# A state-space layer beside a gated MLP: the compute instructions in another order, twelve copies on the other engine

## The chip, the cores and the metric

One Trainium2 chip, one core of it. The core has TensorE (PE, matmuls; PEld is its loading of weights), VectorE (DVE), ScalarE (ACT), GpSimd (POOL) and SyncE (SP, which here only starts transfers). The metric is the device time of one execution in microseconds; lower is better. The time before is a median of three runs; the traces come from one profiled execution.

## The reference

The input is x, 2048 tokens of 512 channels. After a layernorm two branches read it, and both are added to the input:

```python
xn = _layernorm(x, axis=-1)
return x + _A_ref(xn, ...) + _B_ref(xn, ...)

# A: state-space convolution, 128 complex modes for each channel
logdA = dt * A                                  # dt = exp(log_dt)
P = jnp.exp(logdA[:, :, None] * l[None, None, :])
K = jnp.einsum("dn,dnl,dn->dl", Cc, P, dB).real
y = irfft(rfft(u, padded) * rfft(K, padded))[:L] + u * Dskip
# B: gated MLP, F = 1792
h = _sigmoid(x @ w_gate) * (x @ w_up)
return h @ w_down
```

Everything comes in and goes out as bf16.

## The kernel before, in words

The kernel is a plan of 927 numbered operations. An operation is a short Python function that issues one instruction or a few on one engine, or one transfer. `_Plan.add` (L265) numbers them in the order in which the code names them. `_Plan.run` (L291) gives them out in the order of the list `ORDER` (L206), and each engine executes its own in that order, waiting where an input isn't ready. An operation may also take a buffer out of a pool and give one back (`acq`, `rel`); which buffer of the pool it gets is settled by `ORDER` too, first freed, first used. The pool "s" has two pairs of PSUM banks of 128x1024 f32, the pool "gu" four single banks.

`_Plan.copy` (L279) makes a copy that either engine can do: on DVE as `tensor_copy` (L286 in the profile) when its number stands in the tuple `ON_DVE` (L204), else on ACT as an activation (L288). Two other tuples, `UEV` and `ON_ACT`, do the like for other operations; they are the same before and after.

The work, with the numbers that matter here:

- *Layernorm.* Four groups of 512 tokens: statistics on DVE (L542, L543), a small part on POOL (L481, L482, or L492), then `fn2` on DVE (L501, L502) and the scaling on either (L549, L554). Transposed tokens go to `xnT`.
- *Gated MLP.* Four groups of 512 tokens. A gate tile is four matmuls (`fg`, L1045), an up tile four (`fu`, L1069); ACT takes the sigmoid (L1057), up tiles come out through ACT (L1084) or not, and DVE multiplies (L1089, L1094). Then four down-projections of 14 matmuls for each group (L1123).
- *Power tables.* A ladder of squares (L669 on ACT, L676 and L678 on DVE) gives the powers of the modes. In four chunks c of 128 channels tables G and H are filled by complex products on DVE (L737, L738, L742, L743), squares on ACT (L792) and eight small seed copies for each chunk (L777, operations 194 to 201, 240 to 247, 287 to 294, 333 to 340). Matmuls of G with H (L823) give the kernel's samples.
- *The convolution in the frequency domain.* x goes through a first transform (L695), out to a scratch in DRAM and back. Then come two passes p of 256 channels with eight units u each. A unit is: a matmul into a pair (`fm`, L885); an eviction of the pair (L889); a swap of halves into the other half of the partitions, by transfers in pass 0 and for three units of pass 1, and by four DVE copies (L898) for the five others; a matmul of the kernel's spectrum (`fk`, L911) and its eviction (L913); products on DVE (L916, L920); the inverse transform (`fv`, L935) into a pair; its eviction (L939); and a store to the scratch `v_scr`.
- *The end.* When all units are stored, `reload` (L972) reads `v_scr` back in parts: five transfers on SP, two on ACT, and later one more on SP behind a first output store. For the first three groups of tokens `final` (L999) makes 2 x 4 matmuls into a pair (L994), and DVE adds the MLP's part (L1020). For the last group the matmuls go on top of the down-projection in its bank (L994 and L997), and DVE adds the input (L1143); its fourth block is done in two halves. Each result goes out with a transfer.

Around the places that the prediction speaks of, the rows of the engines are these (numbers of operations; p, u are pass and unit):

| engine, place | before | after |
|---|---|---|
| DVE near 155 to 168 us | 430, 445 (L916 of p0 u6, u7), 850, 906 (L1094, L1089), 446 (L920 of p0 u7), 431 (L920 of p0 u6), 498 (L898 of p1 u3), 370, 560 (L898 of p1 u2) | 445, 430, 431, 906, 585, 446, 433, 850, 498, 370, 560 |
| ACT there | 585 (eviction, L889, p1 u7), 571, 882, 874, 433 (eviction, L939, p0 u6), 448 (L939, p0 u7), 497 (L889, p1 u3), 861, 890 | 571, 882, 448, 874, 497, 890 |
| PE there | 873, 570, 584, 881, 892, 432 (`fv` p0 u6), 447 (`fv` p0 u7), 889 (gate), 496 (`fm` p1 u3) | 881, 584, 570, 873, 892, 432, 447, 889, 496 |
| PE in the tail | 908, 911 (down-projection of blocks 1 and 2 of the last group), 832, 829 (finals), 915 (down-projection of block 3), 909, 921, 912, 916, 919 (convolution added to blocks 1, 4, 2, 3, 4), 838, 835, 920, 841, 844, 922 | 908, 911, 829, 832, 909, 912, 915, 916, 919, 838, 835, 920, 841, 844, 921, 922 |

Before as after, 432 writes into the pair that 585 empties, and 496 into the pair that 433 empties.

Of the kernel before, what the change touches and what calls it, by code (L numbers as in the profile page):

```python
# [182 lines left out]
def _consts():  # L183
# [17 lines left out]
                MAB=f(np.stack([quads(MA[by], True), quads(MB[by], True)], axis=2)), E=f(_build_E(M2, by).reshape(128, NU // 2, 2, NKT, 128).transpose(1, 0, 2, 3, 4)))  # L201

UEV = (6, 7, 10, 11, 12, 13, 14, 15, 16, 17, 18, 19, 22, 23, 24, 25, 26, 27, 28, 29, 30, 31, 32, 33, 34, 35, 36, 37, 38, 39, 40, 41, 44, 45, 46, 47, 52, 53, 54, 55,)
ON_DVE = (86, 89, 104, 106, 121, 122, 123, 137, 138, 184, 194, 195, 198, 199, 201,)  # L204
ON_ACT = (2,)
ORDER = [  # L206
# [40 lines left out]

class _Op:
    __slots__ = ("alt", "tab", "eng", "cost", "fn", "prio", "acq", "rel", "dma", "left", "users", "ready", "start", "done", "seq", "mode")
# [8 lines left out]
class _Plan:  # L258
# [20 lines left out]
    def copy(self, nc, cost, out, in_, *args, **kw):  # L279

        get = lambda v: v() if callable(v) else v
        dve = len(self.ops) in ON_DVE

# [35 lines left out]
def kernel(  # L319
# [209 lines left out]
    def layernorm(i0, i1, prio):  # L529
# [15 lines left out]
        for i in range(i0, i1):  # L545
            dve = i < LN_ACT or len(pl.ops) in ON_DVE
            if not dve:
# [110 lines left out]
    def f_cast(cur, k, dve):  # L658
        for p in range(NP):
            if dve:  # L660
                V.tensor_copy(out=W[p][:, k], in_=cur[:, :, DW * p:DW * p + DW])
            else:
                S.activation(out=W[p][:, k], in_=cur[:, :, DW * p:DW * p + DW], func=ACT.Identity)
    cast_prev = [None, None]
    for k in range(12):
        cur = wt[(2 * k) % 3]
        sq, nxt = wt[(2 * k + 1) % 3], wt[(2 * k + 2) % 3]
        if k < 11:
            s_op = pl.add("ACT", 0.95, lambda cur=cur, sq=sq: S.activation(out=sq, in_=cur, func=ACT.Square),  # L669
                          [cur_op] + W_op[-1:], PLAD + k * 0.01)  # L670
        dve = len(pl.ops) in ON_DVE
        c_op = pl.add("DVE" if dve else "ACT", 1.04, lambda cur=cur, k=k, dve=dve: f_cast(cur, k, dve), [cur_op],
# [540 lines left out]
```

## Time and profile before

| | |
|---|---|
| median of 3 runs | 215.39 us (213.83 to 215.43) |
| profiled execution, span from first to last instruction | 213.6 us |
| granted TensorE clock | 1.000 |
| busy: PE, DVE, ACT | 204.2, 191.3, 177.1 us |
| DMA | 42.61 MB, mean 199 GB/s |

A busy PE is not PE at its peak: the end of a matmul is modelled and overlaps the next one. A line of a timeline has the start in us, the time from the first start to the last end of instructions merged in it, engine, line, operation, output and inputs with their shapes, and in brackets the idle time before it with what ended it. A group's line has, behind the bar, busy us and the mean ns of one, and behind the second bar the idle us just before its instructions. A wait's line has the total us, how often, and the longest.

### The profile page before, as it was taken

What the parts mean: (1) busy time and instruction counts of PE and PEld (TensorE: products, weight loads), DVE (VectorE), ACT (ScalarE), POOL (GpSimd) and SP (SyncE); (2) the same over time, 40 slices, a digit from 0 to 9 for tenths busy, and PEclk for the clock granted to TensorE, in tenths of its full rate; (3) what the DMA queues carried; (4) which work ended last, traced back from release to release, by engine and by line L of the source; (5) the groups of instructions that cost most, each with busy time, mean ns of one, the idle gap of its engine ahead of it and who ended that gap; (6) DMA issues with size and microseconds to landing.
All of it is one profiled execution on the core that took longest, in us unless ns stands there. A gap on an engine that the chain in (4) does not pass through costs nothing.

```text
span 213.6 us, 4875 instructions
## 1 busy us (share of the span) xinstructions
PE 204.2 (96%) x1838; PEld 102.9 (48%) x1864; DVE 191.3 (90%) x406; ACT 177.1 (83%) x284; POOL 27.8 (13%) x32
## 2 busy tenths in 40 slices
PE   7989999999999999999999999999999999999992
PEld 2654444444443444445436555544654645644482
DVE  4799999999979999999999999999992999990494
ACT  5699999999999999997999989978989998870000
POOL 2120026008980000002000000001200000000000
PEclk9999999999999999999999999999999999999999
DMA  5999269124464236967965878787967799698864
GB/s 148 316 383 381 100 147 324 61 98 147 110 126 104 76 105 229 213 191 151 249 185 141 228 202 237 215 221 175 202 188 208 217 284 274 141 357 218 240 213 172
DMA packets 52377, 42.61 MB, mean 199 GB/s; under 512 B 16641, under 2 KB 44546, under 8 KB 52354
## 3 DMA queue, kind: packets, MB, share of 16 engines
q1 hardware_dynamic: 50658, 40.30, 63.9%
q0 software_dynamic: 864, 1.57, 4.8%
q10 hardware_dynamic: 832, 0.43, 0.8%
q8 instruction: 14, 0.23, 0.5%
q14 instruction: 9, 0.07, 0.1%
HBM read 24.99 MB, written 12.85 MB: 177 GB/s over the span
## 4 chain that ended last, share of the span: by engine, by line
PE 41%; DVE 40%; POOL 6%; DMA 4%; issue 4%; ACT 3%; DVEq 0%; SPq 0%; ACTq 0%
PE pair L911 8%; PE bank L1045 7%; PE bank L1123 7%; PE bank L1069 7%; DVE big L737 6%; DVE big L738 6%; POOL ln_ve_b L481 5%; PE pair L935 5%; DVE big L742 4%; DVE big L743 4%; DVE stats L542 3%; DVE hT_sb L1094 3%; DVE hT_sb L1089 3%; DVE big L678 2%; DMA big<-v_scr 2%
## 5 line engine op out<-in xcount | busy, mean ns | idle before, releaser
L288 ACT ACTIVATE big<-pair 128x1024 bf16<-128x1024 f32 x64 | 64.5, 1039 | 6.9 <-DVE big L920 1.7
L1069 PE MATMUL bank<-xnT,wu_sb 128*128 128x512 bf16 x214 | 52.9, 379 | 1.7 <-issue 0.6
L1123 PE MATMUL bank<-wd_sb,hT_sb 128*128 128x512 bf16 (+1 forms) x231 | 50.6, 367 | 0.5 <-issue 0.2
L1045 PE MATMUL bank<-xnT,wg_sb 128*128 128x512 bf16 (+1 forms) x191 | 45.6, 370 | 1.0 <-issue 0.5
L1045 PEld LDWEIGHTS <-wg_sb 128*128 128x128 bf16 x240 | 22.5, 98 | 25.0 <-issue 3.2
L1123 PEld LDWEIGHTS <-hT_sb 128*128 128x128 bf16 x238 | 22.4, 98 | 24.9 <-issue 1.6
L1069 PEld LDWEIGHTS <-wu_sb 128*128 128x128 bf16 x224 | 20.7, 98 | 27.5 <-issue 5.4
L1057 ACT ACTIVATE hT_sb<-bank 128x512 bf16<-128x512 f32 x48 | 28.2, 627 | 0.7 <-PE bank L1045 0.7
L737 DVE TENSOR_TENSOR big<-big 128x1024 bf16<-128x1024 bf16 (+4 forms) x40 | 26.7, 667 | 0.2
L738 DVE TENSOR_TENSOR big<-big 128x1024 bf16<-128x1024 bf16 (+4 forms) x40 | 26.5, 663 | 0.0
L1084 ACT ACTIVATE us_sb<-bank 128x512 bf16<-128x512 f32 x40 | 23.6, 616 | 0.6 <-DVE hT_sb L1089 0.3
L911 PE MATMUL pair<-big 128*128 128x256 bf16 x160 | 19.8, 273 | 0.0
L916 DVE TENSOR_TENSOR big<-big 128x2048 bf16<-128x2048 bf16 x16 | 19.3, 1217 | 0.1
L911 PEld LDWEIGHTS <-big 128*128 128x128 bf16 x160 | 15.4, 98 | 4.7 <-issue 0.8
L481 POOL TENSOR_SCALAR ln_ve_b<-mvb 128x4 bf16<-128x4 bf16 x3 | 13.0, 4323 | 34.1 <-DVE mvb L543 34.1
L742 DVE TENSOR_TENSOR big<-big 128x512 bf16<-128x512 bf16 (+4 forms) x40 | 16.5, 413 | 0.2
L743 DVE TENSOR_TENSOR big<-big 128x512 bf16<-128x512 bf16 (+4 forms) x40 | 16.5, 412 | 0.0
L792 ACT ACTIVATE sq_sb<-big 128x256 bf16<-128x256 bf16 (+2 forms) x20 | 13.2, 658 | 1.6 <-DVE big L743 1.5
L1089 DVE TENSOR_TENSOR hT_sb<-hT_sb,us_sb 128x1024 bf16<-128x1024 bf16 x20 | 13.5, 683 | 0.0
L935 PE MATMUL pair<-big 64*64 64x512 bf16 (+1 forms) x256 | 13.1, 327 | 0.0
L898 DVE COPY big<-big 32x1024 bf16<-32x1024 bf16 x20 | 8.4, 418 | 4.5 <-ACT big L288 4.2
L288 ACT ACTIVATE big<-big 128x256 bf16<-128x256 bf16 x30 | 12.4, 452 | 0.0
(99 smaller groups left out, 229.8 us busy)
## 6 DMA issues: line engine op xcount, KB each, us to landing
big<-c_E SPq DMA_DIRECT2D x13, 320.0 KB, 4.4
z_scr<-big SPq DMA_DIRECT2D x16, 256.0 KB, 2.9
big<-z_scr SPq DMA_DIRECT2D x16, 256.0 KB, 4.2
v_scr<-big SPq DMA_DIRECT2D x16, 256.0 KB, 3.2
big<-big SPq DMA_DIRECT2D x44, 64.0 KB, 3.3
big<-in_A_u_dram SPq DMA_DIRECT2D x4, 512.0 KB, 9.1
wu_sb<-in_B_w_up_dram SPq DMA_DIRECT2D x2, 896.0 KB, 10.8
wd_sb<-in_B_w_down_dram SPq DMA_DIRECT2D x1, 1792.0 KB, 9.0
```

Source lines behind the costliest of these rows:

```text
L288: nc.scalar.activation(out=get(out), in_=get(in_), func=ACT.Identity)
L481: P.tensor_scalar(out=q["ve_b"], in0=mvb[:, s, 1], scalar1=EPS, scalar2=None, op0=ALU.add)
L737: V.tensor_tensor(out=wide(outp), in0=wide(lo), in1=mre, op=ALU.mult)
L738: V.tensor_tensor(out=wide(tb()), in0=wide(lo), in1=mim, op=ALU.mult)
L742: V.tensor_tensor(out=outp[:, :, 0], in0=outp[:, :, 0], in1=tb()[:, :, 1], op=opr)
L743: V.tensor_tensor(out=outp[:, :, 1], in0=outp[:, :, 1], in1=tb()[:, :, 0], op=opi)
L911: T.matmul(two(sk)[:, o:o + DW], es()[:, g, kt, :], kTv[p][:, :, kt, :], start=kt in (0, NKT - 1), stop=kt >= NKT - 2)
L935: T.matmul(two(sv)[o:o + 64, DW * (2 * g + y):2 * DW * (g + 1)], mab[b:b + 64, 2 * u + g, q, :], pq()[b:b + 64, q, ch] if y else pp()[b:b ...
L1045: T.matmul(bank(sl, k % 2)[:, c0:c1], w[:, kt, k * 128:(k + 1) * 128], xnT[:, grp, kt, c0:c1], start=(kt == 0), stop=(kt == KT - 1))
L1057: S.activation(out=hT_sb[:, hs.idx, k % 2, :], in_=bank(sl), func=ACT.Sigmoid)
L1069: T.matmul(bank(sl), wu_sb[:, kt, k * 128:(k + 1) * 128], xnT[:, grp, kt, :], start=(kt == 0), stop=(kt == KT - 1))
L1123: T.matmul(bank(po)[:, 0:c[1] - c[0]], hT_sb[:, hts[k // 2].idx, k % 2, jj * 128:(jj + 1) * 128], wd_sb[:, k, c[0]:c[1]], start=first and ...
```

## The change

All operations stay; 12 copies change the engine, and `ORDER` is another permutation of the same 927 numbers. The 168 transfers that SP starts are in the same order as before, and so are those of ACT and POOL among themselves. Of the copies, 198 and 201 go from DVE to ACT; 196, 200, 240, 243, 247, 287, 333, 336 (seeds of the tables H, L777), 433 and 585 go from ACT to DVE. POOL's row differs in one place: the table's constant (193) now stands behind the last layernorm group's part (134).

```diff
-ON_DVE = (86, 89, 104, 106, 121, 122, 123, 137, 138, 184, 194, 195, 198, 199, 201,)
+ON_DVE = (86, 89, 104, 106, 121, 122, 123, 137, 138, 184, 194, 195, 196, 199, 200, 240, 243, 247, 287, 333, 336, 433, 585,)
 ON_ACT = (2,)
 ORDER = [
...
-    444, 902, 867, 429, 361, 511, 513, 348, 340, 865, 362, 419, 430, 445, 363, 557, 510, 365, 873, 868, 850, 364, 366,
-    368, 570, 584, 373, 372, 367, 585, 533, 881, 571, 882, 906, 545, 892, 586, 874, 446, 589, 431, 369, 432, 433, 447,
-    889, 496, 448, 574, 857, 497, 587, 558, 861, 498, 370, 588, 597, 890, 522, 449, 860, 559, 883, 560, 523, 434, 371,
...
+    868, 438, 363, 816, 895, 425, 364, 439, 445, 365, 512, 881, 494, 430, 431, 906, 366, 323, 521, 511, 584, 570,
+    873, 513, 419, 557, 510, 368, 585, 446, 892, 432, 571, 433, 372, 367, 882, 533, 447, 448, 850, 889, 874, 496,
+    558, 545, 586, 497, 498, 890, 589, 369, 370, 559, 560, 860, 857, 861, 883, 884, 522, 523, 590, 574, 587, 588,
...
-    555, 872, 863, 600, 819, 879, 531, 876, 556, 532, 601, 878, 602, 888, 880, 908, 821, 911, 825, 832, 833, 829, 828,
-    824, 826, 915, 909, 921, 822, 823, 830, 831, 827, 912, 916, 910, 919, 838, 834, 835, 913, 917, 914, 839, 836, 920,
-    923, 918, 841, 844, 922, 840, 924, 842, 845, 837, 843, 925, 846, 926]
+    553, 554, 555, 568, 819, 529, 888, 530, 531, 556, 877, 532, 872, 879, 600, 878, 863, 876, 821, 825, 373, 828,
+    880, 601, 908, 911, 829, 602, 824, 830, 826, 822, 832, 833, 909, 912, 823, 910, 915, 913, 916, 917, 831, 827,
+    919, 838, 839, 835, 836, 920, 923, 834, 841, 842, 914, 844, 918, 921, 922, 840, 924, 845, 837, 843, 846, 925,
+    926]
```

69 rows, old and new, of the table ORDER are left out of this document.

## The prediction

> **What bounds the kernel now.** I read the table of stages first, since a busy share over the whole span hides which engine sets the pace where; then the waits, then the timelines of the two places where an engine stands still. In the table each row is a stretch, and an engine's first number is its busy time in it.
>
> ```profile
> PE 204.2 (96%) x1838; PEld 102.9 (48%) x1864; DVE 191.3 (90%) x406; ACT 177.1 (83%) x284; POOL 27.8 (13%) x32
> ```
> ```profile
> core 0: us, PE busy (x) PEld busy (x) DVE busy (x) ACT busy (x) POOL busy (x), PEclk, DMA share, GB/s
> 12.00:112.00 100.00, 98.58 (x749) 44.53 (x758) 98.14 (x231) 97.14 (x169) 23.23 (x18) 1.00 0.61 175
> 112.00:160.00 48.00, 47.42 (x592) 25.69 (x601) 47.62 (x95) 43.34 (x67) 2.26 (x3) 1.00 0.78 202
> 160.00:164.00 4.00, 3.82 (x51) 1.58 (x44) 0.05 (x1) 4.00 (x7) 0.00 (x0) 1.00 0.81 235
> 164.00:190.00 26.00, 25.34 (x257) 14.64 (x261) 25.45 (x42) 22.59 (x28) 0.00 (x0) 1.00 0.83 241
> 190.00:214.00 24.00, 19.37 (x149) 11.27 (x149) 12.21 (x20) 2.32 (x4) 0.00 (x0) 1.00 0.72 218
> ```
> Three engines are full at once. From 12 to 160 us PE, DVE and ACT all work over 90% of the time, at the full clock (1.00). So another order can win only what is idle now, and can lose much more. What PE, the fullest, waited for at its three big groups (the number behind the bar) is small:
>
> ```profile
> L1069 PE MATMUL bank<-xnT,wu_sb 128*128 128x512 bf16 x214 | 52.9, 379 | 1.7 <-issue 0.6 <-ACT hT_sb L1057 0.2 <-DVE hT_sb L1094 0.2
> L1123 PE MATMUL bank<-wd_sb,hT_sb 128*128 128x512 bf16 (+1 forms) x231 | 50.6, 367 | 0.5 <-issue 0.2
> L1045 PE MATMUL bank<-xnT,wg_sb 128*128 128x512 bf16 (+1 forms) x191 | 45.6, 370 | 1.0 <-issue 0.5 <-ACT xnT L572 0.3
> ```
> That is 1.7 + 0.5 + 1.0 = 3.2 us, 1.5% of the span: about the most that an order can take out of PE in the middle. DVE has one hole, in the row 160 to 164 (0.05 busy), while ACT is full there (4.00 of 4.00). In the waits it is the first of these lines, against the longest wait for a neighbour that DVE had before 160 us:
>
> ```profile
> DVE big L898 <- ACT big L288: 4.2, 1, 4.2
> DVE ln_ri_f L501 <- POOL ln_sd_b L482: 1.2, 1, 1.2
> ```
> After the hole DVE runs 25.45 of 26 us without a pause, to the last product of the convolution; then come that unit's last matmul and copy, the store, the reload, and the final adds. So two things set the end: when the exchange copies (L898) after the hole can start, and how the last 15 us are ordered.
>
> **The twelve copies.** Ten of them are small seeds of the power tables (128x256 bf16; 196, 200, 240, 243, 247, 287, 333, 336 to DVE, 198 and 201 to ACT), so DVE gets six more. A seed on DVE shows 0.27, but the next instruction starts 0.13 us later, here at 54.07 behind 53.94:
>
> ```profile
> 53.94 0.27 DVE L286 COPY big<-big 128x256 bf16<-128x256 bf16 x1
> 54.07 1.22 DVE L737 TENSOR_TENSOR big<-big 128x2048 bf16<-128x2048 bf16 x1
> ```
> Six of them cost DVE 6 x 0.13 = 0.8 us (6 x 0.27 = 1.6 at most, nothing if each fell into a gap). I take 0.8, as DVE has almost no gap up to 160 us. It arrives at the hole that much later, and the hole swallows it.
>
> The two others are evictions of a PSUM pair (128x1024 f32): the spectrum of pass 1, unit 7 (585) and the result of pass 0, unit 6 (433). On ACT one is 1.04 us. DVE has never done this one; the nearest rows are an add from such a pair and a copy of bf16 from a pair:
>
> ```profile
> L288 ACT ACTIVATE big<-pair 128x1024 bf16<-128x1024 f32 x64 | 64.5, 1039 | 6.9 <-DVE big L920 1.7 <-PE pair L935 1.2 <-PE pair L885 1.0
> L1020 DVE TENSOR_TENSOR big<-pair,glu_sb 128x1024 bf16<-128x1024 f32 x4 | 4.7, 1216 | 6.5 <-PE pair L994 6.5
> L574 DVE COPY xnT<-pair 128x1024 bf16<-128x1024 bf16 x1 | 0.7, 684 | 0.0
> ```
> So each costs DVE 0.7 to 1.2 us; I take 1.2, since its source is f32 in PSUM as in the add. Both, 2.4 us, stand in DVE's new row exactly before the L898 copy that ends the hole. If the hole were not there they would cost 2.4.
>
> **Through the hole, step by step.** DVE, ACT and PE before:
>
> ```profile
> 155.00 2.35 DVE L916 TENSOR_TENSOR big<-big 128x2048 bf16<-128x2048 bf16 x2
> 157.27 0.68 DVE L1094 TENSOR_TENSOR hT_sb<-hT_sb,bank 128x512 bf16<-128x512 bf16 x1
> 157.86 0.69 DVE L1089 TENSOR_TENSOR hT_sb<-hT_sb,us_sb 128x1024 bf16<-128x1024 bf16 x1
> 158.47 1.29 DVE L920 TENSOR_TENSOR big<-big 128x1024 bf16<-128x1024 bf16 x2
> 163.95 1.71 DVE L898 COPY big<-big 32x1024 bf16<-32x1024 bf16 x4 [4.20 <-ACT big L288]
> ```
> ```profile
> 158.25 1.94 ACT L288 ACTIVATE big<-pair 128x1024 bf16<-128x1024 f32 x2 [0.76 <-PE pair L885]
> 160.07 1.09 ACT L1057 ACTIVATE hT_sb<-bank 128x512 bf16<-128x512 f32 x2
> 161.03 2.89 ACT L288 ACTIVATE big<-pair 128x1024 bf16<-128x1024 f32 x3
> ```
> ```profile
> 159.84 1.49 PE L935 MATMUL pair<-big 64*64 64x512 bf16 x32
> 161.49 0.81 PE L1045 MATMUL bank<-xnT,wg_sb 128*128 128x512 bf16 x3 [0.16 <-issue]
> 162.23 0.41 PE L885 MATMUL pair<-big,m 64*64 64x512 bf16 x4
> ```
> The first of the three ACT copies at 161.03 is 433; it frees the pair into which the L885 matmul of 162.23 (unit 3 of pass 1, 496) writes; the third copies that result (497), and L898 (498) reads it at 163.95. After the change DVE comes to L916 at 155.8 and goes on: the two L916 to 158.1, then L920 of unit 6 (now first) to 158.7, L1089 to 159.3, the eviction 585 to 160.5, the other L920 to 161.1. PE's L935 for unit 6 needs the pair that 585 frees, so it starts at 160.5 instead of 159.84, and ends near 161.3; DVE's eviction 433 runs from there to 162.5; L1094 follows to 163.1. On PE the second L935 ends near 162.0, the gate matmuls (four of 0.215 us) near 162.9, 496 near 163.2. On ACT 497 stands behind the copy 448 and one sigmoid, and runs from 163.4 to 164.4. So L898 starts at about 164.45: 0.5 us later than before, with only some 1.3 us of the hole left. The 2.4 us are hidden, and what ACT is spared (8 seeds, two evictions) does not come through, since the route goes over PE and the same pairs. Bounds: nothing if DVE's eviction takes 0.7, 1.2 if PE's order adds another gate of 0.86. I take +0.5. DVE's next 25 us hold the same instructions; two L898 are moved ahead of one product each, which costs nothing as PE has other matmuls there (25.34 of 26 us) and would cost their 1.7 us without that cover.
>
> **The moves before 155 us.** Nearly all of them swap work that is ready with other work that is ready, on engines that are full anyway. Each could open a small wait or close one; I bound the sum by the longest such wait seen, 1.2 us both ways, and take 0. Counted along the two rows of numbers, PE changes between full-array and small-tile matmuls 75 times before and 74 after, so nothing comes from there.
>
> **The tail.** PE's row behind the last reloads changes. Before: two finals (L994 into pairs), the down-projection of the third block (2.97), then the small L994/L997 groups that add the convolution to the first three blocks. After: those of the first two blocks (909, 912) stand ahead of that down-projection.
>
> ```profile
> 198.67 0.69 PEld L994 LDWEIGHTS <-big 128*64 128x64 bf16 x14 [0.47 <-DMA big<-v_scr]
> 199.78 2.97 PE L1123 MATMUL bank<-wd_sb,hT_sb 128*128 128x512 bf16 x13 [0.16 <-issue]
> 202.68 0.51 PE L994 MATMUL bank<-big 128*64 128x256 bf16 x5
> ...
> 208.16 1.70 PE L1123 MATMUL bank<-wd_sb,hT_sb 128*128 128x256 bf16 x14
> ```
> ```profile
> 199.23 2.36 DVE L1020 TENSOR_TENSOR big<-pair,glu_sb 128x1024 bf16<-128x1024 f32 x2 [6.50 <-PE pair L994]
> 203.34 1.94 DVE L1143 TENSOR_TENSOR big<-bank,big 128x512 bf16<-128x512 f32 x3 [1.76 <-PE bank L997]
> 210.06 0.41 DVE L1143 TENSOR_TENSOR big<-bank,big 128x256 bf16<-128x256 f32 x1
> ```
> They read the last columns of the reload, the third of SP's five reloads, which was issued in the window of the first row below; the second row is how long v_scr's transfers took:
>
> ```profile
> big<-v_scr SPq DMA_DIRECT2D x1, 384.0 KB
> ```
> ```profile
> DMA to landing us min/median/max: 2.6/4.8/7.2
> ```
> Issued at about 194.6 and with 6 us (between median and longest), it lands at 200.6; PE is there at 199.6. So PE waits 1.0 us (0 to 2.2) with 2.97 us of ready work queued behind. What comes back: two of DVE's three L1143 are done under the down-projection, so 1.3 us of the 7.1 that DVE runs from 203.34 to its end are gone from the last stretch. PE's last 7.2 us (202.68 to 209.86) shrink by what the two groups took, to 6.1 to 6.6. I take +0.4 (from -0.6 to +1.6).
>
> **The sum.** 0 before 155 us, +0.5 at the hole, +0.4 in the tail: the profiled span of 213.6 us becomes 214.5. The runs' median of 215.39 stands 1.8 us above that span, and I leave that distance: 215.39 + 0.9 = 216.3 us. Bounds of the terms: -1.2 + 0 - 0.6 = -1.8 and 1.2 + 1.2 + 1.6 = +4.0, hardly all at once; the forecast's own range is 215.0 to 217.4.
>
> **Rivals.**
> *DVE comes late, slower.* The two evictions are hidden only while the hole is there. If DVE reaches it more than 1.3 us later than I say, by waits that the new row opens before 155 us, each further microsecond of the 2.4 falls on the 25.45 us behind it. At the worst 2.4 + 0.9 = 3.3: about 218.6 us. For it: DVE is the fuller engine (47.62 against ACT's 43.34 in 112 to 160) and gets the work. Against it: the size of the hole. The Trainium skill, "Perfetto Trace Analysis", section "Optimizing Scalar/DVE Operations", says that work may be given to ScalarE when DVE is saturated; this change gives it the other way, so by that rule this case would be the likeliest, with the same 218.6; the stage table agrees that DVE is saturated, except in the hole where the two stand.
> *ACT's relief comes through, faster.* ACT is full in the hole; without two copies, 2 x 0.9 us of its row, unit 3's copy could end 1.8 us earlier, and the reload land as much earlier. PE then waits 0.5 less for it (0.47 in the row at 198.67), and only if PE also loses 1.9 of its 3.2 us of waits does the sum reach -2.4: 213.0 us. Against it: the pairs that the route has to pass.
> *The wait on POOL goes, no change to be seen.* Before, a tiny POOL instruction took 11 us and ended when DVE had nothing left:
>
> ```profile
> 48.64 11.08 POOL L481 TENSOR_SCALAR ln_ve_b<-mvb 128x4 bf16<-128x4 bf16 x1 [12.95 <-DVE mvb L543]
> 58.55 1.08 DVE L738 TENSOR_TENSOR big<-big 128x1792 bf16<-128x1792 bf16 x1
> ```
> If it gets through sooner in the new row, DVE saves its 1.2: 215.1 us. The Trainium skill, "SBUF — State Buffer", section "Who interferes with whom", has the second of the two blocked whole while a DVE instruction with two SBUF inputs runs; between the statistics and their reader the new row has again only such work, so by that rule the wait stays and the sum is mine.
> *The change doesn't do what it says.* The planner runs the row as written, but if the waits fall where they fell, nothing moves: 215.4 us.
>
> **How the numbers follow.** Forecast 0.45, DVE late 0.28, ACT's relief 0.12, POOL 0.10, nothing 0.05. Over 1% is 2.2 us, about what a measurement of this kernel can tell from no change. Then faster 0.12, within 1% 0.60, slower 0.28. The range takes in both outer cases' prices: 213.0 to 218.7 us.
>
> **What would show it.** Right: DVE's wait before the first L898 shrinks from 4.2 to about 1.3 us and L898 starts within 1 us of 164; two DVE copies out of pairs of about 1.2 us stand before it; PE waits near 200 us on a DMA out of v_scr before a bank L994; PE's big groups keep some 3 us of idle. Wrong: L898 starts after 166 or before 163, PE's idle at those groups doubles or halves, or the two evictions take 0.7.

## The result, and the profile after

Run on the same chip, the changed kernel takes 217.01 us (median of 20 runs, 215.69 to 219.6) and the kernel before 215.32 us (213.83 to 216.9): ratio 1.0074, 95% interval 1.0051 to 1.0097, some 1.6 us slower. The profiled span went from 213.6 to 215.2 us. The forecast was 216.3, and the change is within 1%; but the sum that gave it is right in one term out of three, as the experiments show. Each trace is one execution: that of the changed kernel stands at its median, some of the others up to 2.4 us off theirs (evict_back 220.38 against 218.04, reader_later 213.81 against 214.56), so positions are best read against an earlier place that both traces share.

The profile after begins, like the one before, with the busy times and the table of stages (in each row the length of the stretch, then busy us and instructions of PE, its weight loads, DVE, ACT and POOL, the granted clock, the DMA share and GB/s):

```profile
PE 204.5 (95%) x1839; PEld 103.4 (48%) x1864; DVE 194.6 (90%) x414; ACT 174.1 (81%) x276; POOL 20.8 (10%) x32
```
```profile
core 0: us, PE busy (x) PEld busy (x) DVE busy (x) ACT busy (x) POOL busy (x), PEclk, DMA share, GB/s
12.00:112.00 100.00, 98.95 (x751) 45.36 (x762) 99.28 (x235) 96.77 (x166) 16.21 (x18) 1.00 0.61 176
112.00:160.00 48.00, 46.76 (x587) 25.64 (x593) 47.69 (x95) 41.89 (x65) 2.25 (x3) 1.00 0.75 197
160.00:164.00 4.00, 3.95 (x49) 1.69 (x48) 2.51 (x4) 2.31 (x4) 0.00 (x0) 1.00 0.87 228
164.00:190.00 26.00, 25.29 (x251) 14.59 (x257) 24.92 (x41) 22.76 (x28) 0.00 (x0) 1.00 0.82 243
190.00:216.00 26.00, 20.18 (x165) 11.47 (x159) 12.77 (x21) 3.02 (x4) 0.00 (x0) 0.98 0.67 205
```

PE and DVE are about as full as before up to 160 us, ACT a little less (41.89 of 48 us, 43.34 before). DVE's hole is half filled (2.51 of 4 us, 0.05 before), and ACT has become half idle there (2.31, 4.00 before).

The waits (total us, how often, longest) that answer to those shown of before:

```profile
DVE big L900 <- ACT big L290: 1.2, 1, 1.2
DVE big L288 <- issue: 0.9, 1, 0.9
DVE big L1145 <- PE bank L999: 2.7, 1, 2.7
PE bank L996 <- DMA big<-v_scr: 1.1, 1, 1.1
```

Line numbers are two higher after the change, as `ORDER` is two lines longer. DVE's 4.2 us before the exchange copies have become 1.2 and 0.9; its 1.24 us for POOL are gone; new are PE's wait for the reload, and 2.7 us instead of 1.76 on DVE in the tail.

The hole itself, in the timelines of DVE and ACT:

```profile
158.88 1.22 DVE L288 CAST big<-pair 128x1024 bf16<-128x1024 f32 x1
161.55 1.22 DVE L288 CAST big<-pair 128x1024 bf16<-128x1024 f32 x1 [0.85 <-issue]
164.60 1.72 DVE L900 COPY big<-big 32x1024 bf16<-32x1024 bf16 x4 [1.24 <-ACT big L290]
```
```profile
162.14 1.02 ACT L290 ACTIVATE big<-pair 128x1024 bf16<-128x1024 f32 x1 [1.69 <-PE pair L937]
163.54 1.03 ACT L290 ACTIVATE big<-pair 128x1024 bf16<-128x1024 f32 x1
```

The two evictions take 1.22 us each, the copy 497 starts at 163.54 (worked out: 163.4), the exchange at 164.60 (164.45; before 163.95).

How late PE is, is best read where both orders have done the same matmuls. The weight loads of `f_k` mark two such places: the first chunk's near 79 us, the last chunk's near 155. Before, then after:

```profile
78.94 0.69 PEld L823 LDWEIGHTS <-big 128*32 128x32 bf16 x65 [0.42 <-ACT big L288]
...
155.04 1.37 PEld L823 LDWEIGHTS <-big 128*32 128x32 bf16 x128 [0.42 <-DVE big L742]
156.48 0.55 PEld L1045 LDWEIGHTS <-wg_sb 128*128 128x128 bf16 x4
```
```profile
78.41 0.12 PEld L825 LDWEIGHTS <-big 128*32 128x32 bf16 x2 [0.50 <-ACT big L290]
...
155.29 0.10 PEld L825 LDWEIGHTS <-big 128*32 128x32 bf16 x2 [0.42 <-DVE big L744]
155.56 1.21 PEld L825 LDWEIGHTS <-big 128*32 128x32 bf16 x114 [0.17 <-issue]
156.99 0.17 PEld L825 LDWEIGHTS <-big 128*32 128x32 bf16 x12 [0.23 <-issue]
157.24 0.55 PEld L1047 LDWEIGHTS <-wg_sb 128*128 128x128 bf16 x4
```

At 79 us the changed kernel is 0.53 us ahead, at 155 us 0.25 behind, behind the last `f_k` 0.76 (157.24 against 156.48), and at L900 0.65. So the hole cost nothing more: what is missing at L900 was missing when PE came to it. Half a microsecond went inside the last `f_k` itself: from its first load to the next gate PE takes 1.95 us instead of 1.44, with gaps that the trace puts down to no other engine. Part of it is the execution and not the order: x came 0.5 us later in this one (DVE waited 3.4 us for it, 2.9 before; with the same start of the row it was 2.9 again in tail_back, below).

The tail on PE:

```profile
198.81 0.30 PE L996 MATMUL pair<-xnT,big 128*64 128x256 bf16 x2
...
201.46 0.41 PE L996 MATMUL bank<-big 128*64 128x256 bf16 x3 [1.07 <-DMA big<-v_scr]
...
202.56 2.97 PE L1125 MATMUL bank<-wd_sb,hT_sb 128*128 128x512 bf16 x13 [0.16 <-issue]
205.46 0.52 PE L996 MATMUL bank<-big 128*64 128x256 bf16 x5
...
209.97 1.70 PE L1125 MATMUL bank<-wd_sb,hT_sb 128*128 128x256 bf16 x14
```

The finals begin 0.72 us later than before (198.81 against 198.09), the last down-projection 1.81 (209.97 against 208.16). The tail has lost the difference, 1.09 us: the 1.07 of the wait, whole.

### The profile page after: what moved, and what is told of

The parts are those of the page before. It is cut to its first block, busy times and chain, and to the rows that moved or that the text cites. A ratio compares the mean times of both kernels' runs of the same rounds, so it can differ in the third digit from the quotient of the medians.

```text
span 215.2 us, 4877 instructions
## 1 busy us (share of the span) xinstructions
PE 204.5 (95%) x1839; PEld 103.4 (48%) x1864; DVE 194.6 (90%) x414; ACT 174.1 (81%) x276; POOL 20.8 (10%) x32
## 5 line engine op out<-in xcount | busy, mean ns | idle before, releaser
L1125 PE MATMUL bank<-wd_sb,hT_sb 128*128 128x512 bf16 (+1 forms) x231 | 49.5, 366 | 0.8 <-issue 0.6
L1071 PEld LDWEIGHTS <-wu_sb 128*128 128x128 bf16 x224 | 21.2, 98 | 25.5 <-issue 2.6
L1059 ACT ACTIVATE hT_sb<-bank 128x512 bf16<-128x512 f32 x48 | 29.2, 641 | 1.8 <-PE bank L1047 1.7
L1086 ACT ACTIVATE us_sb<-bank 128x512 bf16<-128x512 f32 x40 | 25.4, 653 | 0.0
L918 DVE TENSOR_TENSOR big<-big 128x2048 bf16<-128x2048 bf16 x16 | 19.4, 1222 | 0.1
L937 PE MATMUL pair<-big 64*64 64x512 bf16 (+1 forms) x256 | 13.1, 327 | 0.4 <-ACT big L290 0.2
L544 DVE BATCH_NORM_STATS2 stats<-big 128x6 f32<-128x512 bf16 x15 | 9.8, 681 | 3.4 <-DMA big<-in_A_u_dram 3.4
L671 ACT ACTIVATE big<-big 128x1024 f32<-128x1024 f32 x11 | 12.1, 1103 | 0.0
L665 ACT ACTIVATE big<-big 128x512 bf16<-128x512 f32 x20 | 11.9, 675 | 0.2 <-DVE big L680 0.2
```

The lines of the kernel that those rows point to most:

```text
L918: V.tensor_tensor(out=pp().rearrange("p q h m -> p (q h) m"), in0=xx().rearrange("p q h m -> p (q h) m"), in1=kb()[:, 0:2 * DW].unsqueeze( ...
L937: T.matmul(two(sv)[o:o + 64, DW * (2 * g + y):2 * DW * (g + 1)], mab[b:b + 64, 2 * u + g, q, :], pq()[b:b + 64, q, ch] if y else pp()[b:b ...
L1059: S.activation(out=hT_sb[:, hs.idx, k % 2, :], in_=bank(sl), func=ACT.Sigmoid)
L1071: T.matmul(bank(sl), wu_sb[:, kt, k * 128:(k + 1) * 128], xnT[:, grp, kt, :], start=(kt == 0), stop=(kt == KT - 1))
L1086: eus.append(pl.add("ACT", 0.48, lambda sl=sl, us=us, kk=kk: S.activation(out=us_sb[:, us.idx, kk % 2, :], in_=bank(sl), func=ACT.Identity ...
L1125: T.matmul(bank(po)[:, 0:c[1] - c[0]], hT_sb[:, hts[k // 2].idx, k % 2, jj * 128:(jj + 1) * 128], wd_sb[:, k, c[0]:c[1]], start=first and ...
```

## The experiments

Each ratio is to the kernel before, run beside it on the same chip; its median was 214.99 us for tail_back, tail_two_groups, evict_back and first_half, 215.05 for evict_only, two_groups_back, seeds_back and pool_cast, and 215.23 for the other four. 0.001 is 0.2 us.

### The tail

*tail_back*: the last 50 operations in the order of before. On PE:

```diff
-908, 911, 829, 832, 909, 912, 915, 916, 919, 838, 835, 920, 841, 844, 921, 922
+908, 911, 832, 829, 915, 909, 921, 912, 916, 919, 838, 835, 920, 841, 844, 922
```

> The changed kernel, but the last 50 operations of the row (from the down-projections of the last group on, near 192 us) in the order of before; all else as changed. Theory A, the tail costs the whole wait: PE is what ends the program, so the two small groups that were moved ahead of the third down-projection cost the same 1.1 us there as behind it, nothing comes back, and the wait of 1.1 to 1.3 us for the last columns is lost whole. Then this kernel is 1.1 to 1.3 us faster than the changed one: 0.3 to 0.6 us over the kernel before (ratio 1.001 to 1.003), and PE waits 0.3 us or less for v_scr. Rival B, the sum of the prediction, in which 0.6 of the 1.0 us came back: only 0.4 us faster than the changed one, 1.2 us over the kernel before (ratio 1.0055). Rival C, the tail is late only because what comes before it is late: no gain, ratio 1.007.

Measured: 1.0013 (0.9995 to 1.0031), 0.6% or 1.3 us less than the changed kernel. Its tail:

```profile
199.79 3.20 PE L1125 MATMUL bank<-wd_sb,hT_sb 128*128 128x512 bf16 x14
202.91 0.52 PE L996 MATMUL bank<-big 128*64 128x256 bf16 x5
...
208.39 1.70 PE L1125 MATMUL bank<-wd_sb,hT_sb 128*128 128x256 bf16 x14
```

The small groups stand at 202.91 again, the wait of 1.07 is gone, and the last down-projection starts at 208.39 instead of 209.97: 1.58 us earlier, of which 0.49 was there when the finals began (198.32 against 198.81), and 1.09 is the tail.

*tail_two_groups*: the kernel before with two operations of PE moved.

```diff
-    824, 826, 915, 909, 921, 822, 823, 830, 831, 827, 912, 916, 910, 919, 838, 834, 835, 913, 917, 914, 839, 836, 920,
+    824, 826, 909, 912, 915, 921, 822, 823, 830, 831, 827, 916, 910, 919, 838, 834, 835, 913, 917, 914, 839, 836, 920,
```

> The kernel before with one edit: the small matmul groups that add the convolution to blocks 1 and 2 of the last group (909, 912) stand ahead of the third down-projection (915); every other engine's row is as before. Theory A: PE waits 0.8 to 1.3 us near 200 us for the reload of v_scr with the ready 2.97 us down-projection behind it, and the end moves by as much: 0.8 to 1.3 us slower than before (ratio 1.004 to 1.006). Rival B: about 0.4 us slower (ratio 1.002), since two of DVE's three additions go under the down-projection and PE's last stretch shrinks. Rival D: the wait is smaller than in the changed kernel, as the rest of the tail's row is another; then below 0.3 us.

Measured: 1.0050 (1.0021 to 1.0079), 1.1 us slower.

*two_groups_back*: the changed kernel with 915 ahead of the two again.

```diff
-    880, 601, 908, 911, 829, 602, 824, 830, 826, 822, 832, 833, 909, 912, 823, 910, 915, 913, 916, 917, 831, 827,
+    880, 601, 908, 911, 829, 602, 824, 830, 826, 822, 832, 833, 915, 909, 912, 823, 910, 913, 916, 917, 831, 827,
```

> The changed kernel with one matmul group moved: the third down-projection of the last group (915) stands ahead of the two small groups 909 and 912 again; every other row is as changed. Theory A, these two groups alone are the tail's loss: 0.9 to 1.3 us faster than the changed kernel (ratio to before 1.001 to 1.003), and PE waits for v_scr 0.3 us or less. Rival B, they cost 0.4 us: ratio 1.0055. Rival J, other moves of the tail (the start of the adds' matmuls 921 for the last block, two finals in the other order) carry half of it: ratio 1.004.

Measured: 1.0034 (1.0007 to 1.0061), 0.9 us less than the changed kernel. Theory A holds in tail_back, where 1.0055 and 1.007 lie outside the interval. In tail_two_groups its price is met, and theory B's 1.002 lies just outside. two_groups_back can't choose: 1.0034 lies between theory A's and rival J's 1.004, and even B's 1.0055 is inside the interval. So the new tail costs 1.3 us, of which the two groups are 0.9 to 1.1; what the rest of its order costs isn't resolved.

### The two evictions

*evict_back*: the changed kernel with both on ACT.

```diff
-ON_DVE = (86, 89, 104, 106, 121, 122, 123, 137, 138, 184, 194, 195, 196, 199, 200, 240, 243, 247, 287, 333, 336, 433, 585,)
+ON_DVE = (86, 89, 104, 106, 121, 122, 123, 137, 138, 184, 194, 195, 196, 199, 200, 240, 243, 247, 287, 333, 336,)
```

> The changed kernel with the two evictions 433 and 585 back on ACT, at their places in the changed row; nothing else differs. Theory A, the hole hides them on DVE, and ACT has no use for the time: within 0.3 us of the changed kernel, DVE's wait before the first of the four-copy swaps near 164 us is about 2 us longer and ACT is full from 160 to 164. Rival E, DVE is the bound and comes late: without 2.4 us of work on DVE the kernel is 0.5 to 2.4 us faster than the changed one. Rival F, ACT is the bound there: putting the two back costs up to 1.8 us, and the kernel is slower than the changed one by 0.5 to 1.8 us.

Measured: 1.0116 (1.0092 to 1.0139), 0.9 us more than the changed kernel. Two rows of it, PE's and DVE's:

```profile
162.69 1.02 PE L1047 MATMUL bank<-xnT,wg_sb 128*128 128x512 bf16 x4 [0.96 <-ACT hT_sb L1059]
```
```profile
165.22 1.71 DVE L900 COPY big<-big 32x1024 bf16<-32x1024 bf16 x4 [5.16 <-issue]
```

With 433 and 585 on it, ACT comes late with a sigmoid (162.05, in the changed kernel 159.86), a gate waits 0.96 for its bank, and the exchange starts at 165.22 instead of 164.60, though the last `f_k` was level (155.18 against 155.29). Theory A fails in its second half, and rival F's price is met with 0.9 of its 0.5 to 1.8. Its reason, an ACT that is full, isn't what the trace shows: ACT stands still 0.64 us for PE's result ahead of 433 (161.13), and the sigmoid stands behind 433 in this row. On DVE, 433 is out of the sigmoid's way.

*evict_only*: the kernel before with only these two on DVE, 431 behind 445 and 585 behind 850.

```diff
-ON_DVE = (86, 89, 104, 106, 121, 122, 123, 137, 138, 184, 194, 195, 198, 199, 201,)
+ON_DVE = (86, 89, 104, 106, 121, 122, 123, 137, 138, 184, 194, 195, 198, 199, 201, 433, 585,)
```

> The kernel before with only the two evictions 433 and 585 on DVE, in the row 430, 445, 431, 850, 585, 906, 446, 433, 498; the rows of PE and SP are those of before. Theory A, the hole hides them and ACT's relief does come through, since putting them back into the changed kernel cost it 0.4 to 1 us: the four-copy swaps start at about 163.5 instead of 163.95 and the kernel is 0.3 to 0.6 us faster than before (ratio 0.997 to 0.9985). Rival I, the relief was worth something only in the changed row, where ACT comes to the hole with other work: within 0.2 us of before. Rival E, DVE is the bound: 0.5 to 2.4 us slower (ratio 1.002 to 1.011).

Measured: 0.9978 (0.9951 to 1.0005), 0.5 us faster. As expected in size, but the interval just includes 1. The place was not as expected. DVE:

```profile
160.99 1.23 DVE L288 CAST big<-pair 128x1024 bf16<-128x1024 f32 x1
164.01 1.71 DVE L900 COPY big<-big 32x1024 bf16<-32x1024 bf16 x4 [1.80 <-ACT big L290]
```

The exchange starts at 164.01, no earlier than before (163.95), though the last `f_k` had started 0.18 later (155.22 against 155.04): 0.12 us is won between the two. Where the rest of the half microsecond comes out isn't shown; that the hole hides the evictions is.

### The ten seed copies

*seeds_back*: tail_back with the ten on the engines of before.

```diff
-ON_DVE = (86, 89, 104, 106, 121, 122, 123, 137, 138, 184, 194, 195, 196, 199, 200, 240, 243, 247, 287, 333, 336, 433, 585,)
+ON_DVE = (86, 89, 104, 106, 121, 122, 123, 137, 138, 184, 194, 195, 198, 199, 201, 433, 585,)
```

> The kernel with the changed order and the tail of before (its ratio was 1.0013), with the ten seed copies back on the engines of the kernel before: eight on ACT again, two on DVE. Theory K, the six more copies cost DVE 0.13 us each and DVE is the bound: 0.5 to 0.8 us faster than that kernel, ratio 0.9975 to 0.999. Theory A, up to the hole the engines take turns in being late and the hole takes up what DVE is late: within 0.3 us of it, ratio 1.000 to 1.0025. For POOL: if the copies on DVE are what lets POOL's instructions through, its second one near 55 us takes longer than 5.75 us without the copy at 54, and DVE waits 0.5 us or more for it; if the two type casts at 57 are enough, nothing changes there.

Measured: 1.0114 (1.0072 to 1.0156), 2.2 us more than tail_back. Theory K fails in sign, theory A in size. Two of its waits, and the first `f_k` on PE:

```profile
ACT big L290 <- PE pair L825: 2.3, 2, 1.2
DVE big L739 <- ACT big L290: 1.3, 2, 0.7
```
```profile
79.12 1.44 PE L825 MATMUL pair<-big 128*32 128x82 bf16 x128 [0.84 <-DVE big L288]
```

DVE's products wait twice for seeds that ACT copies, 0.58 us for one copied at 57.38 and 0.72 for two copied at 80.60. Those two stand behind PE's first `f_k`, for which ACT waits 1.21. That `f_k` is itself 1.1 us later than in tail_back (77.98): its matmuls wait for seed 201, which DVE copies at 78.70 and ACT had copied at 77.19. So in the new order ACT comes to some of these copies too late, and DVE to one that the change had given to ACT.

*seeds_only*: the kernel before, order unchanged, with the ten on the engines of the change.

```diff
-ON_DVE = (86, 89, 104, 106, 121, 122, 123, 137, 138, 184, 194, 195, 198, 199, 201,)
+ON_DVE = (86, 89, 104, 106, 121, 122, 123, 137, 138, 184, 194, 195, 196, 199, 200, 240, 243, 247, 287, 333, 336,)
```

> The kernel before, its order unchanged, with only the ten seed copies on the engines of the changed kernel (six more on DVE). Taking them back out of the changed order cost 1 % (ratio 1.0114 against 1.0013). Theory N, a seed is 0.13 us of DVE's row against 0.31 us of ACT's and DVE needs it early, so DVE is the better engine for it in any order: 0.3 to 1 us faster than before (ratio 0.995 to 0.9985). Theory O, the loss came only because in the changed order the seeds stand at places that suit DVE, and ACT came to them late; in the order of before ACT has them in time: DVE pays 0.8 us, part of it hidden in the hole, ratio 1.000 to 1.004.

Measured: 1.0054 (1.0031 to 1.0077), 1.2 us slower, a little above theory O. ACT's wait for DVE's products in the kernel before, then that wait, the hole and the last `f_k` here:

```profile
ACT sq_sb L792 <- DVE big L743: 1.5, 4, 0.5
```
```profile
ACT sq_sb L794 <- DVE big L745: 4.1, 8, 1.1
DVE big L900 <- ACT big L290: 4.2, 1, 4.2
```
```profile
155.97 0.10 PEld L825 LDWEIGHTS <-big 128*32 128x32 bf16 x2 [0.51 <-DVE big L744]
```

DVE's row has six copies more, 0.8 us at 0.13 each, and DVE comes to the two L918 (L916 before) ahead of the hole 1.17 us later (156.17 against 155.00). ACT's squares wait 4.1 us in eight waits for DVE's products instead of 1.5 in four, and PE comes to the last `f_k` at 155.97 instead of 155.04. The hole is still 4.2 us long: it moved with the rest instead of taking the lateness up. Theory O was right in sign, but its "part of it hidden in the hole" is refuted.

*copies_only*: the order of before, evict_only's row of DVE, and all twelve copies moved.

```diff
-ON_DVE = (86, 89, 104, 106, 121, 122, 123, 137, 138, 184, 194, 195, 198, 199, 201,)
+ON_DVE = (86, 89, 104, 106, 121, 122, 123, 137, 138, 184, 194, 195, 196, 199, 200, 240, 243, 247, 287, 333, 336, 433, 585,)
```

> All twelve copies on the engines of the changed kernel, in the order of before, with the DVE row of the kernel in which only the two evictions were moved (its ratio was 0.9978): the half of the change that is not the order. By theory N both gains add up: ratio 0.993 to 0.9965. By theory O the evictions' 0.5 us remain and the seeds take 0 to 0.8 us of it back: ratio 0.998 to 1.0015.

Measured: 1.0033 (1.0003 to 1.0062). The parts multiply to that: 1.0054 x 0.9978 = 1.0032. Theory N falls. Theory O is right in sign, but its range of 0.998 to 1.0015 is missed, as the seeds' price is 1.2 instead of 0 to 0.8.

### The order up to the hole, and POOL

*first_half*: the changed order and its seeds up to about 123 us, the order of before from there. `ORDER` at the seam, against the changed one's:

```diff
-751, 314, 482, 402, 455, 460, 315, 487, 461, 403, 758, 383, 757, 384, 380, 488
+751, 314, 402, 757, 482, 315, 455, 758, 487, 380, 383, 460, 316, 760, 761, 405
```

> The changed order and the ten moved seed copies up to about 123 us, the order of before from there on (the hole and the tail as before, both evictions on ACT). In the two traces the matmuls stand level at 123 us, although x came 0.47 us later in the changed kernel's execution. Theory A, the first half wins something, since DVE no longer waits 1.24 us for POOL near 60 us, and the late x was that execution alone: 0.3 to 0.6 us faster than before (ratio 0.997 to 0.9985). Rival G, it wins nothing, the ten copies cost DVE 0.8 us and the wait on POOL only hid them: ratio 1.000 within 0.001. Rival H, x comes later because of the order: 0.3 to 0.5 us slower than before (ratio 1.0015 to 1.0025).

Measured: 1.0026 (1.0005 to 1.0046). Not what theory A said, but it tells little. The number is close to rival H's (1.0015 to 1.0025), whose reason doesn't hold: DVE waits 3.4 us for x here and in the changed kernel and 3.3 in two_groups_back, but 2.9 in tail_back and combined, all with the same start of the row. PE at the seam:

```profile
125.70 1.25 PE L913 MATMUL pair<-big 128*128 128x256 bf16 x10 [0.37 <-ACT big L290]
```

A `fk` matmul waits there for an ACT row that is in neither kernel. A splice has a price of its own, and the 0.37 of this one is more than half of the effect.

*combined*: the changed order up to 152 us, then evict_only's order, all twelve copies moved. PE's row at the seam, against the kernel before's:

```diff
-428, 864, 867, 363, 365, 873, 570, 584, 881, 892, 432, 447, 889, 496
+428, 417, 864, 849, 891, 363, 365, 873, 570, 584, 881, 892, 432, 447, 889, 496
```

> The changed order and its ten seeds up to about 152 us, then the order of before with the two evictions on DVE, and the tail of before. If the parts add up: the first part is 0.25 us ahead of before at 155 us in the traces, the evictions on DVE bring 0.5, the tail costs nothing: 0.6 to 0.9 us faster than before (ratio 0.996 to 0.997), the fastest of all so far. Rival P, what a seam costs (0.5 us in the kernel spliced at 123 us) takes it back: ratio 0.998 to 1.000.

Measured: 1.0009 (0.9981 to 1.0037), nearest to rival P; the sum of the parts, 0.996 to 0.997, lies outside. It is 0.23 us ahead of before at 155 us, then loses 0.7 in one gap of `f_k`:

```profile
154.81 0.10 PEld L825 LDWEIGHTS <-big 128*32 128x32 bf16 x2 [0.42 <-DVE big L744]
155.08 1.16 PEld L825 LDWEIGHTS <-big 128*32 128x32 bf16 x114 [0.18 <-issue]
156.94 0.17 PEld L825 LDWEIGHTS <-big 128*32 128x32 bf16 x12 [0.71 <-issue]
```

*pool_cast*: tail_back with DVE's cast 86 and the copy 199 behind the reader of POOL's result. DVE's row near 56 to 62 us:

```diff
-195, 190, 86, 212, 199, 213, 698, 136
+195, 190, 212, 213, 698, 136, 86, 199
```

> The kernel with the changed order and the tail of before (ratio 1.0013), with the two type casts (operation 86) and the copy that reads them (199) moved behind the reader of POOL's result (136), so that from 56 us to that reader DVE runs only products with two inputs in SBUF. Theory L, POOL's tiny instructions come through while DVE runs an instruction with one input: then POOL's second one ends only when DVE has nothing left, DVE waits 0.8 to 1.3 us for it near 60 us as it did before the change, and the kernel is up to 1 us slower (ratio 1.002 to 1.006). Rival M, they came through because they were started later, at another place of DVE's row: no wait, POOL's second one still takes 5 to 6 us, ratio 1.001.

Measured: 1.0032 (1.0007 to 1.0056; the 1.001 of rival M is inside), and no wait of DVE. POOL, and DVE's last copy and the product that runs when POOL ends:

```profile
53.49 1.11 POOL L483 TENSOR_SCALAR ln_ve_b<-mvb 128x4 bf16<-128x4 bf16 x1 [14.76 <-DVE mvb L545]
54.68 4.95 POOL L484 TENSOR_TENSOR ln_sd_b<-ln_ve_b,half 128x4 bf16<-128x4 bf16 x1
```
```profile
55.83 0.28 DVE L288 COPY big<-big 128x256 bf16<-128x256 bf16 x1
...
59.31 0.62 DVE L745 TENSOR_TENSOR big<-big 128x896 bf16<-128x896 bf16 x1
```

POOL is done at 59.63, with nothing but two-input products on DVE behind that copy. Theory L's wait doesn't come, so it falls. The products leave one small pause, 1.13 us from 57.64 to the next at 58.77 where the same product took 1.00 before it; whether that let POOL in isn't shown.

*reader_later*: the kernel before with one product ahead of the reader.

```diff
-    717, 691, 84, 670, 143, 146, 707, 160, 699, 135, 165, 708, 673, 684, 681, 85, 212, 136, 671, 213, 138, 124,
+    717, 691, 84, 670, 143, 146, 707, 160, 699, 135, 165, 708, 673, 684, 681, 85, 212, 213, 136, 671, 138, 124,
```

> The kernel before with one edit of DVE's row: the product 213 (two instructions, 1.2 us) stands ahead of the reader of POOL's result (136) instead of behind it. In all rows so far POOL's two tiny instructions ended between 58.2 and 61.4 us, whenever they were started (48.6 or 53.5 to 53.9). Theory M, POOL is done at a time that does not hang on when DVE pauses, and the changed row only has other work of DVE ahead of the reader: DVE's wait of 1.2 us is gone, POOL's pair still ends at about 60.5, the kernel is 0 to 0.5 us faster than before (ratio 0.9975 to 1.000). Theory L, POOL's instruction comes through only when DVE has nothing left: the wait stays at 1.2 us, only later, and POOL's first instruction takes 12.3 us; ratio 1.000.

Measured: 0.9978 (0.9954 to 1.0002), 0.5 us faster, with the interval just reaching 1. Its POOL, DVE's reader and the last `f_k`:

```profile
48.65 0.57 POOL L483 TENSOR_SCALAR ln_ve_b<-mvb 128x4 bf16<-128x4 bf16 x1 [12.78 <-DVE mvb L545]
49.31 1.33 POOL L484 TENSOR_TENSOR ln_sd_b<-ln_ve_b,half 128x4 bf16<-128x4 bf16 x1
```
```profile
60.76 0.17 DVE L503 RECIPROCAL ln_ri_f<-ln_sd_b 128x4 f32<-128x4 bf16 x1
```
```profile
153.89 1.37 PEld L825 LDWEIGHTS <-big 128*32 128x32 bf16 x128 [0.42 <-DVE big L744]
```

The wait of 1.24 us is gone and PE comes to the last `f_k` 1.15 us earlier (153.89 against 155.04). The runs say 0.5; how the rest of that 1.15 comes about isn't shown. But theory M's reason, a POOL that ends near 60 us anyway, is wrong as well: here it was done at 50.6.

Two versions came out 0.5 us faster than the kernel before, evict_only and reader_later, each with an interval that just includes 1. They touch different stretches; the two together were not tried.

## Why the prediction was right, and where it wasn't

In parts, from the ratios: the twelve copies in the old order cost 0.7 us (copies_only 1.0033; seeds +1.2, evictions -0.5). The new order up to 190 us gives 0.4 back (tail_back 1.0013). The new tail costs 1.3 (1.0074 less 1.0013). Together 1.6; each part has some 0.5 us of uncertainty, only the tail and the seeds stand clear of it.

- *The bound.* Right that three engines are full. That its 3.2 us of idle were "about the most that an order can take out of PE in the middle" was a misreading. The groups of tail_back:

```profile
L1071 PE MATMUL bank<-xnT,wu_sb 128*128 128x512 bf16 x224 | 53.6, 379 | 0.1
L1125 PE MATMUL bank<-wd_sb,hT_sb 128*128 128x512 bf16 (+1 forms) x238 | 50.6, 367 | 0.0
L1047 PE MATMUL bank<-xnT,wg_sb 128*128 128x512 bf16 (+1 forms) x200 | 47.1, 371 | 0.0
```

  All 224, 238 and 200 matmuls are there, with 0.1 us of idle. The rows of before had x214, x231 and x191: 26 records are missing, and a lost first record of a tile looks like a wait of 0.16 with "issue" as its cause, as at 161.49 (gate, x3 of 4). reader_later and tail_two_groups, whose rows on PE are that of before up to the tail, also have all 662, with 0.4 and 0.7 us of idle. So most of the 3.2 us were such holes in the record.
- *The seeds, 0.8, swallowed by the hole.* The step that failed: "It arrives at the hole that much later, and the hole swallows it." In the old order the size was near (1.2 us), the cover was not there. In the changed order, for which it was forecast, even the sign is wrong: with the ten copies moved the kernel is 2.2 us faster than without (seeds_back). In the old order, before 160 us, ACT's squares and PE's `f_k` wait for DVE's table, so what DVE is late makes all three late (PE at 155.97 against 155.04), and the hole, which ends when ACT and PE bring their result, moves along.
- *The evictions.* 1.22 us each (taken: 1.2), both hidden: right. "what ACT is spared (8 seeds, two evictions) does not come through" failed for the evictions: 0.9 us in the changed order, about 0.5 in the old one. The rival "ACT's relief" had the sign of this; it was priced too high by far.
- *The hole, +0.5.* The route came out within 0.3 us (eviction 161.55, 497 at 163.54, exchange at 164.60, wait 1.24), but not by the step "PE's L935 for unit 6 needs the pair that 585 frees, so it starts at 160.5". 585 was done at 160.10, and PE came to L937 at 160.59 right behind its gate matmuls (158.76 to 160.66). The lateness was on PE already at 157.24; as a term of the hole it is 0.
- *The moves before 155 us, 0 with 1.2 either way.* Held: between the two traces 0.25 late, 0.3 early in tail_back, where x came in time.
- *The tail, +0.4.* The wait was 1.07 (forecast 1.0). The step that failed: "What comes back: two of DVE's three L1143 are done under the down-projection", with PE's last stretch 0.6 to 1.1 us shorter. It did shrink, from 7.18 us (202.68 to 209.86) to 6.21 (205.46 to 211.67), but by the two groups' own work, which PE had paid ahead of the down-projection. On the engine that sets the end, moving work forward wins nothing, so the term was the wait whole, 1.1, where 0.4 stood.
- *The wait on POOL.* Given 0.10, and it did go, as the products 213 and 698 came ahead of the reader. The ground against it does not hold. The new row has not only products with two inputs there: the cast 86 and the copy 199 stand among them. And with the same row of DVE, POOL's instruction took 11.08 us from 48.64 (before) and 0.57 from 48.65 (reader_later). The Trainium skill, "SBUF — State Buffer", section "Who interferes with whom", has whichever of the two issues first hold the shared pair of ports for the whole instruction; which of them that was, and why it differed, these runs don't show.

So that the forecast came within 0.7 us (216.3 against 217.01, or 0.9 of slowing against 1.6) is luck, as misses offset: 0.9 too little in the tail, 0.5 too much at the hole, and 0.3 net of copies and order where 0 stood. Most of the signs that were to show it right came true (DVE's wait of 1.24, the exchange at 164.60, two copies of 1.22, PE's wait near 200 us): they show that these steps took place, not what each costs.

## What to carry to other kernels

A hole on one engine hides work only if it stands in the hole: work put ahead of it delays what the other engines wait for, and the hole moves along. On the engine that sets the end, pulling work ahead of ready work costs the whole wait for its input and brings nothing back. Count a group's records before its idle time is read, and compare two orders only at places where both have done the same work.

## What the runs showed of the hardware beside that

- A seed copy (128x256 bf16) is 0.13 us of DVE's row and 0.45 us long on ACT (12.4 us for 30), yet which engine is better for the same ten changed sign with the order: +1.2 us for DVE in the old, 2.2 us in its favour in the new.
- Inside the 128 loads of the last `f_k`, a gap of 0.23 to 0.71 us ahead of the last 12 shows in the changed kernel, tail_back, two_groups_back and combined, and not in before, seeds_only, evict_back or pool_cast, though evict_back has the changed kernel's row of PE. The profile names no cause; it stays open.
